# Parallel block (sliding attention and GEGLU): the first chunk reordered, stacks loaded sooner, another bank tag, an h tile loaded sooner

## The chip, the cores and the metric

The kernel runs on one core of one Trainium2 chip. A time is the device time of one execution in microseconds (us); the figure for a kernel is the median of its runs. In the profile PE is TensorE's matmuls, PEld its weight loads, DVE is VectorE, ACT ScalarE, POOL GpSimd, SP the engine that issues the DMAs (its queue is SPq). PEclk is the clock that TensorE was granted, 1.00 being full speed.

## The reference

A transformer block whose two branches run in parallel on one normalised input, in float32, with S = 2048 tokens, D = 640, 32 heads of 20, and a hidden width of 1728:

```python
xn = _layernorm(x, axis=-1)
return x + _A_ref(xn, A_wqkv, A_wo) + _B_ref(xn, B_w_gate, B_w_up, B_w_down)

# A: attention, each query sees the 256 latest keys
qkv = (xn @ wqkv).reshape(B, S, 3, H, Dh).transpose(2, 0, 3, 1, 4)
scores = einsum("bhqd,bhkd->bhqk", q, k) * Dh ** -0.5
mask = (idx[:, None] - idx[None, :] >= 0) & (idx[:, None] - idx[None, :] < 256)
p = softmax(where(mask, scores, -1e9));  a = (p @ v) @ wo
# B: GEGLU
h = gelu(xn @ w_gate) * (xn @ w_up);     b = h @ w_down
```

## The kernel before

Every dense product in float32 is made of three: an operand is split into a high part (rounded by ACT to TensorE's fast float format) and a low part (the rest, by a subtraction on DVE or GpSimd), and high·high, low·high and high·low are summed in one bank of PSUM (`dense_steps`, L79 to L84). So nearly every tile costs an ACT copy, a subtraction, and three matmuls for each block of 128.

The work is staged. Tokens are taken in four chunks of 512 (four tiles `xi` of 128 tokens).

1. **First chunk** (`first_chunk`, from L286): statistics of each tile on DVE (L119 to L121), variance plus epsilon (`ve`, L126), square root on ACT (`sq`, L127), a short DVE chain for the reciprocal root (L132 to L135), the normalisation (`ln_apply`, L139), the transposes on PE (`turn`, L156), then the high half of the transposed tile `xh` on ACT (L292) and the low half `xl` on DVE (L289). The chunk goes in two halves of 256 tokens, `ta` from tiles 0 and 1, `tb` from tiles 2 and 3. Meanwhile the weights of q and k of the first column blocks (`wr0`, `wr5`) are split: `wqh` on ACT (L74), `wql` on GpSimd (L75). PE's products are grouped in `part` (L296), five matmuls each. The weights of v are split as they come (`wvh`, L238, ACT; `wvl`, L239, GpSimd), and then come the projections `proj_v` and `proj_qk` (L82). Each projection of q or k is stored by `save_qk`: the evictions L215 and L216, L203 on ACT, the subtraction `pt` on GpSimd (L204, two buffers), and its stores on SP (L210).
2. **Chunks 1 to 3**: `ln_scale` (L141), `ln_turn`, `proj_v` and `proj_qk` of the chunk before. The statistics of chunk 1 are taken inside the first chunk.
3. **Attention** (`attention`): 32 units, one for each group of four heads and each chunk, of 14 slots each. In each slot the schedule issues score products, maxima, exponentials, the products with v, and some matmuls of a list of filler (the rest of the q, k and v projections, and gate and up products `gate_up_fill`). `load_stack` (L390) loads a unit's stacks of q (`qs`, three buffers) and k (`ks`, four buffers) from DRAM by six DMAs; `max_end` stores the maxima into the stack of q (L427).
4. **Gate and up products** of the remaining columns (`gate_up` and `gate_up_pair`), where products of sums of x and weights save some matmuls. Results `he` go to DRAM (`hd`) by L884 and L886.
5. **Down and output projections** (`terms`, L941): `load_step` (L900) loads an h tile, `split_step` splits it (L918 on ACT, L920 on GpSimd).

The order on PE, ACT and DVE is the order of the program in most of this (`manual_schedule` with the engines of `MANUAL`, SP too in stages 4 and 5); on an engine that isn't named there, GpSimd and SP in the stages before, a scheduler places the instructions. Before the change the attention's loads stand at the start of a unit:

```python
for u in range(NU + 1):
    if 1 <= u and u + 2 < NU:
        load_stack(u + 2)
```

The pool `psg` gives each tag ("g0" to "g3", two buffers each) its place in PSUM; the pools of the attention that held the same banks are closed before, so the first product in a bank waits for the bank's last reader.

Of the kernel before, what the change touches and what calls it, by code (L numbers as in the profile page):

```python
# [9 lines left out]
F32 = mybir.dt.float32  # L10
F32R = mybir.dt.float32r
BF = mybir.dt.bfloat16
AF = mybir.ActivationFunctionType
OP = mybir.AluOpType
# [31 lines left out]
def block_kernel(ctx, tc, x, xt, wqk, wv, wo, wgu, wd, wdl, out):  # L46
# [3 lines left out]
    dram = ctx.enter_context(tc.tile_pool(name="dram", bufs=1, space=DRAM))  # L50

    one = const.tile([128, 96], F32, name="one")
    nc.vector.memset(one, 1.0)
    nc.scalar.activation(one, one, AF.Sqrt)
    ident = const.tile([128, 128], F32, name="ident")
    make_identity(nc, ident)
    edge = ctx.enter_context(tc.tile_pool(name="edge", bufs=1, side="right"))
# [39 lines left out]
    vp = pr.enter_context(tc.tile_pool(name="vp", bufs=5, side="right"))  # L97
    st1 = pr.enter_context(tc.tile_pool(name="st1", bufs=1, side="right"))
    identb = st1.tile([128, 256], BF, name="identb")[:, 0:128]
    mask = st1.tile([128, 384], F32, name="mask")  # L100
    nc.gpsimd.memset(mask, 0.0)
    nc.gpsimd.affine_select(out=mask, in_=mask, pattern=[[1, 384]], compare_op=OP.is_ge,
# [14 lines left out]
    def ln_stats(xi, mv, lp):  # L117
        st = lp.tile([128, 2, 6], F32, name="st", tag="st", bufs=4)
        nc.vector.bn_stats(st[:, 0, :], xi[:, 0:320])  # L119
        nc.vector.bn_stats(st[:, 1, :], xi[:, 320:640])  # L120
        nc.vector.bn_aggr(mv, st)  # L121

    def ln_sqrt(mv, n, lp):
        ve = lp.tile([128, n], F32, name="ve", tag="ve", bufs=2)
        sq = lp.tile([128, n], F32, name="sq", tag="sq", bufs=2)
        nc.vector.tensor_scalar(ve, mv[:, :, 1], EPS, None, op0=OP.add)  # L126
        nc.scalar.activation(sq, ve, AF.Sqrt)  # L127
        return ve, sq

    def ln_rstd(ve, sq, n, lp):  # L130
# [154 lines left out]
    def first_chunk(xs, wr0, wr5, lp):  # L285
        halves = slice(0, 256), slice(256, 512)  # L286

        def low(k, ps, cs):
            nc.vector.tensor_tensor(out=xl[:, k, cs], in0=ps, in1=xh[:, k, cs].bitcast(F32), op=OP.subtract)  # L289

        def high(k, ps, cs):
            nc.scalar.activation(xh[:, k, cs], ps, AF.Copy)  # L292

        def part(ps, w, r, cs, first=False, last=False):
            for k in range(KT):
                nc.tensor.matmul(ps[:, cs], w[:, k, :], r[:, k, cs], start=first and k == 0,  # L296
                                 stop=last and k == KT - 1, skip_group_check=True)

        with tc.manual_schedule(engines=MANUAL):
            mv = [lp.tile([128, 2, 2], F32, name="mv", tag="mv", bufs=2) for _ in range(2)]  # L300
            ln_stats(xs[0], mv[0][:, 0, :], lp)
            ln_stats(xs[1], mv[0][:, 1, :], lp)
            va = ln_sqrt(mv[0], 2, lp)
            ln_stats(xs[2], mv[1][:, 0, :], lp)
            rs = ln_rstd(*va, 2, lp)
            ln_apply(xs[0], mv[0][:, 0, :], rs[:, 0:1])
            ln_apply(xs[1], mv[0][:, 1, :], rs[:, 1:2])
            ln_stats(xs[3], mv[1][:, 1, :], lp)
            w0 = split_qk(wr0)
            w5 = split_qk(wr5)  # L310
            ta = [turn(k, xs[0:2], "xmxmm"[k]) for k in range(KT)]
            dn = [psd.tile([128, C], F32, name="ps_d", tag="dn") for _ in range(2)]
            for k in range(KT):
                high(k, ta[k], halves[0])
                if k == 1:
                    vb = ln_sqrt(mv[1], 2, lp)
            for k in range(2):
                low(k, ta[k], halves[0])
            rs = ln_rstd(*vb, 2, lp)
            ln_apply(xs[2], mv[1][:, 0, :], rs[:, 0:1])  # L320
            ln_apply(xs[3], mv[1][:, 1, :], rs[:, 1:2])
            part(dn[0], w0[0], xh, halves[0], True)
            part(dn[1], w5[0], xh, halves[0], True)
            part(dn[0], w0[1], xh, halves[0])
            tb = [turn(0, xs[2:4], "o")]
            for k in range(2, KT):
                low(k, ta[k], halves[0])
            for k in range(1, 3):
                tb.append(turn(k, xs[2:4], "oxmxm"[k]))
            part(dn[1], w5[1], xh, halves[0])  # L330
            for k in range(3, KT):
                tb.append(turn(k, xs[2:4], "oxmxm"[k]))
            for k in range(KT):
                high(k, tb[k], halves[1])
            for k in range(KT):
                low(k, tb[k], halves[1])
            mv = lp.tile([128, 4, 2], F32, name="mv4", tag="mv4", bufs=2)
            for i, w in enumerate((w0, w5)):
                part(dn[i], w[0], xl, halves[0])
                part(dn[i], w[0], xh, halves[1])  # L340
                part(dn[i], w[1], xh, halves[1])
                part(dn[i], w[0], xl, halves[1], last=True)
                for j in range(2):
                    ln_stats(xs[4 + 2 * i + j], mv[:, 2 * i + j, :], lp)
                save_qk(5 * i, 0, dn[i])
        return w0, w5, mv

    v0 = []
    with tc.tile_pool(name="lp", bufs=1, side="right") as lp:
        xs = [ln_load(t, lp) for t in range(4)]  # L350
        warm = lp.tile([128, 256], BF, name="warm")[:, 0:128]
        nc.vector.memset(warm, 0.0)
        ps = psd.tile([128, C], F32, name="ps_u", tag="dn")
        for i in range(WARM):
            nc.tensor.matmul(ps[:, 0:128], warm, warm, start=True, stop=True)
        wr0, wr5 = load_qk(0), load_qk(5)
        prep = load_v(0, v0, lp)
        next(prep)
        xs += [ln_load(t, lp) for t in range(4, 8)]
        w0, w5, mv1 = first_chunk(xs, wr0, wr5, lp)  # L360
        nc.vector.tensor_copy(identb, ident)
        run(prep)
        v0 = v0[0]
        ones = lp.tile([2, 2 * C], BF, name="ones")
        nc.gpsimd.memset(ones, 1.0)
        for i in range(NK):
            for j in (0, 2):
                nc.sync.dma_start(ks[i][120:122, j:j + 2].rearrange("p j t -> p (j t)"), ones)
        for c in range(1, NC):
            ln_scale(xs[4 * c:4 * c + 4], lp, mv1 if c == 1 else None)  # L370
            ln_turn(4 * c, xs[4 * c:4 * c + 4])
            if c + 1 < NC:
                xs += [ln_load(t, lp) for t in range(4 * c + 4, 4 * c + 8)]
            if c == 2:
                raws1 = [load_qk(1), load_qk(6)]
            if c < NC - 1:
                run(*[proj_v(v0, 4 * c - 4 + i, None if i % 2 else (pso, "o")) for i in range(4)])
                run(proj_qk(0, w0, c), proj_qk(5, w5, c))
# [296 lines left out]
    def attention():  # L675
        now[0] = -1
        load_stack(0)
        load_stack(1)
        load_stack(2)
        for i, (p, k, half) in enumerate((p, k, half) for p in range(NC // 2) for k in range(2) for half in range(2)):  # L680
            for j, fn in enumerate(x_sums(p, k, half)):
                at(XS0 + XSN * i + 2 * j, fn)
        for i in range(12):
            now[0] = i - 13
            for fn, a in tick():
                fn(*a)
            for _ in range(2):
                pull_max(1, now[0])
                pull_fill(RAMP)
        pull_fill(GAP)  # L690
        for u in range(NU + 1):
            if 1 <= u and u + 2 < NU:
                load_stack(u + 2)
            for i in range(NS):
                T = now[0] = NS * u + i
                for fn, a in tick():
                    fn(*a)
                if i == 0 and u:
                    av_unit(u - 1)
                if i % 2 == 0:  # L700
                    if u < NU and i < 12:
                        exp_piece(u, i)
                        exp_piece(u, i + 1)
                    pull_max(3 if i in (6, 12) else 2, T)
                pull_fill(RATE / NS)
        while acts:
            now[0] += 1
            for fn, a in tick():
                fn(*a)
        now[0] = None  # L710
        run(fill)
        assert not acts
# [247 lines left out]
    for fn in w_sums(raws_w, sums):  # L960
        fn()
    w = tiles, sums
    gate_up(rest[0], 1, "g0")
    split_xs(0, 2, xraw[2])
    xraw[4] = load_xs(0, 4)
    gate_up(rest[0], 3, "g1")
    split_xs(0, 1, xraw[1])
    later = {2: load_xs(1, 2)}
    gate_up(rest[0], 0, "g2")
    split_xs(0, 3, xraw[3])  # L970
    later[1] = load_xs(1, 1)
    gate_up(rest[0], 2, "g3")
# [48 lines left out]
    for j, f in enumerate(range(NFA, NF - 1)):  # L1021
# [33 lines left out]
        if end:  # L1055
            for n in range(2):
                load_step(n)
            second[1].append(lambda: split_step(0))
            second[2].append(lambda: split_step(1))
        gate_up_pair(f, w, 1, second)  # L1060
        if end:
            load_step(2)
        else:
            w = nxt_w[0], sums
    order.__exit__(None, None, None)
    order = tc.manual_schedule(engines=MANUAL_OUT)
# [72 lines left out]
```

## Time and profile before

| | |
|---|---|
| median of 3 runs | 1113.44 us (1112.27 to 1115.75) |
| the profiled execution | 1111.94 us |
| its span | 1110.2 us |
| granted TensorE clock, mean | 0.998 |
| PE busy | 1091.4 us, 98% |
| DVE, ACT, POOL busy | 54%, 42%, 37% |
| first chunk | to about 24.5 us |
| chunks 1 to 3 | to about 64 us |
| attention with its filler | to about 660 us |
| gate and up products | to about 845 us |
| down and output projections | to the end |

A timeline row gives start and busy time in us, engine, line, operation, tile written and read, their shapes and the number of instructions grouped in the row; in brackets stands the engine's idle time ahead of it and what ended that. A row of waits gives the line that waited, what it waited for, and the waits' total, number and longest.

### The profile page before, as it was taken

Reading aid. Unit: us, or ns where it says so; the run is one execution under the profiler, and the core shown is the slowest. Engines: PE = TensorE matmul, PEld = TensorE weight load, DVE = VectorE, ACT = ScalarE, POOL = GpSimd, SP = SyncE. Lnnn points to the kernel's source line nnn. Section 1 sums busy time; section 2 is a strip of 40 time slices with the busy share of each in tenths; the row PEclk is TensorE's granted clock in tenths of the full one; section 3 lists DMA queues with packets and bytes.
Section 4 is the critical chain, followed back from the end, with each engine's and each line's share of the span. In section 5 each row is a group of like instructions: output and inputs, shape, how many; then the busy total and the mean of one; then the engine's idle time right before and its main releaser. Section 6 shows DMA issues by size and latency. Waiting matters only on the chain.

```text
span 1110.2 us, 19224 instructions
## 1 busy us (share of the span) xinstructions
PE 1091.4 (98%) x6778; PEld 831.3 (75%) x6778; DVE 602.4 (54%) x1646; ACT 469.2 (42%) x952; POOL 411.1 (37%) x568
## 2 busy tenths in 40 slices
PE   7999999999999999999999999999999999999998
PEld 7887666666678767666666768888887888788886
DVE  7856567565666566676666636666653350211203
ACT  4434655565644556554555555232233322211111
POOL 4144544566735435664424341111113313221230
PEclk9999999999999999999999999999999999999999
DMA  4642342446442233444333125122124735152431
GB/s 162 221 140 83 106 151 89 134 120 195 123 132 85 79 119 107 139 135 131 101 101 103 57 82 187 68 92 87 66 74 150 262 130 169 48 180 78 150 95 66
DMA packets 76144, 133.09 MB, mean 120 GB/s; under 512 B 12800, under 2 KB 33664, under 8 KB 76048
## 3 DMA queue, kind: packets, MB, share of 16 engines
q1 hardware_dynamic: 76048, 131.87, 37.7%
q8 instruction: 53, 0.87, 0.3%
q14 instruction: 43, 0.35, 0.1%
HBM read 86.31 MB, written 44.83 MB: 118 GB/s over the span
## 4 chain that ended last, share of the span: by engine, by line
PE 93%; DVE 3%; DMA 1%; ACT 1%; issue 1%; SPq 0%; POOL 0%; DVEq 0%; ACTq 0%
PE ps_d L82 25%; PE ps_w L941 22%; PE ps_g L850 15%; PE ps_o L484 7%; PE ps_e L462 7%; PE ps_m L410 7%; PE ps_v L82 6%; PE ps_g L82 1%; DVE junk L412 1%; PE ps_t L156 1%; PE ps_d L296 1%; DMA ks<-kd 0%; DMA xi<-x 0%; ACT P L464 0%; PE ps_b L911 0%
## 5 line engine op out<-in xcount | busy, mean ns | idle before, releaser
L412 DVE CUSTOM_DVE_ANT_0 junk<-ps_m,mask 128x384 bf16<-128x384 f32 (+2 forms) x512 | 271.8, 531 | 176.4 <-PE ps_m L410 135.3
L464 ACT ACTIVATE P<-ps_e 128x512 f32<-128x512 f32 (+2 forms) x384 | 197.6, 568 | 62.3 <-PE ps_e L462 55.4
L470 POOL TENSOR_SCALAR_AFFINE_SELECT P<-P 128x512 f32<-128x512 f32 x128 | 84.7, 662 | 174.6 <-ACT P L464 169.2
L920 POOL TENSOR_TENSOR ht<-hr,ht 128x512 fp32r<-128x512 f32 x52 | 69.5, 1342 | 173.2 <-ACT ht L918 173.2
L82 PE MATMUL ps_d<-xh,wql 128*128 128x512 f32 x430 | 129.2, 410 | 0.0
L82 PE MATMUL ps_d<-xl,wqh 128*128 128x512 f32 x430 | 128.6, 408 | 0.0
L82 PE MATMUL ps_d<-xh,wqh 128*128 128x512 f32 x430 | 128.5, 409 | 0.0
L410 PE MATMUL ps_m<-ks,qs 120*128 120x128 bf16 (+1 forms) x704 | 121.0, 275 | 3.3 <-DVE mx L412 2.2
L462 PE MATMUL ps_e<-qs,ks 122*128 122x128 bf16 (+2 forms) x704 | 112.9, 277 | 1.0 <-ACT P L464 0.4
L918 ACT ACTIVATE ht<-hr 128x512 fp32r<-128x512 f32 x56 | 35.1, 629 | 132.9 <-PE ps_w L941 80.7
L462 PEld LDWEIGHTS <-ks 122*128 122x128 bf16 x704 | 50.1, 98 | 54.3 <-issue 44.0
L82 PEld LDWEIGHTS ps_d<-xh,wql 128*128 128x128 f32 x430 | 77.9, 189 | 15.5 <-issue 1.9
L82 PEld LDWEIGHTS ps_d<-xl,wqh 128*128 128x128 f32 x430 | 78.2, 188 | 14.8 <-issue 0.4
L82 PEld LDWEIGHTS ps_d<-xh,wqh 128*128 128x128 f32 x430 | 77.8, 189 | 14.1 <-ACT xh L164 0.3
L410 PEld LDWEIGHTS <-qs 120*128 120x128 bf16 x704 | 62.0, 98 | 32.8 <-issue 13.3
L473 POOL TENSOR_SCALAR_AFFINE_SELECT P<-P 128x512 f32<-128x512 f32 x112 | 72.2, 655 | 35.1 <-ACT P L464 35.1
L484 PE MATMUL ps_o<-P,v 128*32 128x384 f32 (+2 forms) x1408 | 84.3, 386 | 0.0
L204 POOL TENSOR_TENSOR pt<-r,pt 128x512 bf16<-128x512 f32 x40 | 46.7, 1166 | 83.0 <-ACT pt L203 80.2
L484 PEld LDWEIGHTS ps_o<-P,v 128*32 128x32 f32 x1408 | 40.1, 110 | 39.5 <-issue 29.2
L75 POOL TENSOR_TENSOR wql<-wr,wqh 128x640 fp32r<-128x640 f32 x11 | 17.8, 1626 | 135.8 <-PE ps_g L850 106.1
L922 DVE TENSOR_TENSOR ht<-hr,ht 64x512 fp32r<-64x512 f32 x4 | 2.8, 691 | 112.3 <-ACT ht L918 112.3
L488 ACT ACTIVATE ob<-ps_o 128x512 f32<-128x512 f32 x32 | 19.1, 597 | 103.6 <-PE ps_o L484 53.2
(269 smaller groups left out, 2040.2 us busy)
## 6 DMA issues: line engine op xcount, KB each, us to landing
hd<-he SPq DMA_DIRECT2D x52, 256.0 KB
hr<-hd SPq DMA_DIRECT2D x52, 256.0 KB
wr<-wgu SPq DMA_DIRECT2D x27, 320.0 KB
qs<-qd SPq DMA_DIRECT2D x32, 240.0 KB
ks<-kd SPq DMA_DIRECT2D x32, 240.0 KB
xi<-x SPq DMA_DIRECT2D x16, 320.0 KB
qs<-qd SPq DMA_DIRECT2D x32, 160.0 KB
ks<-kd SPq DMA_DIRECT2D x32, 160.0 KB
```

The costliest lines, as they stand in the source:

```text
L82: nc.tensor.matmul(ps, a(k), b(k), start=n == 0, stop=n == 3 * nk - 1)
L204: nc.gpsimd.tensor_tensor(out=pt[:, l, :], in0=r, in1=pt[:, 1, :], op=OP.subtract)
L410: nc.tensor.matmul(ps[:, lo:hi], lh, rhs, start=True, stop=True)
L412: nc.vector.tensor_tensor_reduce(out=junk[:, 0:n], in0=ps[:, 0:n], in1=mask[:, 384 - n:384], scale=1.0, scalar=NEG, op0=OP.add, op1=OP.max ...
L462: nc.tensor.matmul(ps[:, col:col + n], k[0:QROWS, j, kc:kc + 128], q[0:QROWS, j, q0:q0 + n], start=True, stop=True)
L464: nc.scalar.activation(pt[:, j, lo:hi], ps[:, lo:hi], AF.Exp, scale=SCALE)
L470: nc.gpsimd.affine_select(out=a, in_=a, pattern=[[0, 4], [1, 128]], compare_op=OP.is_ge, fill=0.0, base=0, channel_multiplier=-1)
L473: nc.gpsimd.affine_select(out=a, in_=a, pattern=[[0, 4], [-1, 128]], compare_op=OP.is_ge, fill=0.0, base=-1, channel_multiplier=1)
L484: nc.tensor.matmul(o[32 * j:32 * j + 32, q0:q0 + n], v[:, w0_:w0_ + 32], pt[:, j, col:col + n], start=i == 0, stop=i == len(todo) - 1, ski ...
L850: nc.tensor.matmul(ps, i, j, start=first and n == 0, stop=n == len(work) - 1, skip_group_check=True)
L920: nc.gpsimd.tensor_tensor(out=t[:, 1, :], in0=raw, in1=t[:, 0, :].bitcast(F32), op=OP.subtract)
L941: nc.tensor.matmul(pss[m], w[:, ms], r, start=first and j == 0, stop=last and j == len(work) - 1)
```

## The change

Four edits.

*First chunk.* The epsilon gets a tile of its own (a part of the constant tile `one`). The square root takes the variance itself, with the epsilon as its bias, while `ve` is made by an addition of two tiles. The statistics of tiles 2 and 3 move behind the normalisation of tiles 0 and 1. ACT's evictions and weight copies are interleaved in a new order, with the second square root behind the third eviction. GpSimd's order is written out too in this function, and its subtractions `wql` stand behind a copy of one column of the normalised fourth tile into `one`. On PE the transposes of the second half go ahead of all the products with `wql`, and those ahead of the last. The bfloat16 copy of the identity moves from DVE to GpSimd, and to the program's start.

*Stacks.* `load_stack(u + 3)` is called in slot 11 of unit u, where `load_stack(u + 2)` was called at slot 0 of unit u (so a unit's stacks are asked for three slots sooner).

*Bank.* The first `gate_up` uses the tag "g2" and the third "g0".

*h tile.* `load_step(2)` is called before the last product of the last `gate_up_pair` rather than behind that function.

```diff
-    nc.vector.memset(one, 1.0)
-    nc.scalar.activation(one, one, AF.Sqrt)
+    nc.vector.memset(one[:, 0:92], 1.0)
+    nc.scalar.activation(one[:, 0:92], one[:, 0:92], AF.Sqrt)
+    eps = one[:, 92:96]
+    nc.vector.memset(eps, EPS)
...
+    nc.gpsimd.tensor_copy(identb, ident)
...
-        nc.vector.tensor_scalar(ve, mv[:, :, 1], EPS, None, op0=OP.add)
-        nc.scalar.activation(sq, ve, AF.Sqrt)
+        nc.vector.tensor_tensor(out=ve, in0=mv[:, :, 1], in1=eps[:, 0:n], op=OP.add)
+        nc.scalar.activation(sq, mv[:, :, 1], AF.Sqrt, bias=eps[:, 0:1])
...
+        def high_qk(raw):
+            wh = wp.tile([128, KT, 128], F32R, name="wqh", tag="wqh")
+            nc.scalar.activation(wh, raw, AF.Copy)
+            return wh
+
+        def low_qk(raw, wh):
+            wl = wp.tile([128, KT, 128], F32R, name="wql", tag="wql")
+            nc.gpsimd.tensor_tensor(out=wl, in0=raw, in1=wh.bitcast(F32), op=OP.subtract)
+            return wh, wl
+
-        with tc.manual_schedule(engines=MANUAL):
+        with tc.manual_schedule(engines=MANUAL | {mybir.EngineType.Pool}):
             mv = [lp.tile([128, 2, 2], F32, name="mv", tag="mv", bufs=2) for _ in range(2)]
             ln_stats(xs[0], mv[0][:, 0, :], lp)
             ln_stats(xs[1], mv[0][:, 1, :], lp)
-            va = ln_sqrt(mv[0], 2, lp)
-            ln_stats(xs[2], mv[1][:, 0, :], lp)
-            rs = ln_rstd(*va, 2, lp)
+            rs = ln_rstd(*ln_sqrt(mv[0], 2, lp), 2, lp)
             ln_apply(xs[0], mv[0][:, 0, :], rs[:, 0:1])
             ln_apply(xs[1], mv[0][:, 1, :], rs[:, 1:2])
+            ln_stats(xs[2], mv[1][:, 0, :], lp)
             ln_stats(xs[3], mv[1][:, 1, :], lp)
-            w0 = split_qk(wr0)
-            w5 = split_qk(wr5)
             ta = [turn(k, xs[0:2], "xmxmm"[k]) for k in range(KT)]
             dn = [psd.tile([128, C], F32, name="ps_d", tag="dn") for _ in range(2)]
-            for k in range(KT):
+            high(0, ta[0], halves[0])
+            wh0 = high_qk(wr0)
+            high(1, ta[1], halves[0])
+            wh5 = high_qk(wr5)
+            high(2, ta[2], halves[0])
+            vb = ln_sqrt(mv[1], 2, lp)
+            for k in (3, 4):
                 high(k, ta[k], halves[0])
-                if k == 1:
-                    vb = ln_sqrt(mv[1], 2, lp)
...
-            part(dn[0], w0[0], xh, halves[0], True)
-            part(dn[1], w5[0], xh, halves[0], True)
-            part(dn[0], w0[1], xh, halves[0])
+            part(dn[0], wh0, xh, halves[0], True)
+            part(dn[1], wh5, xh, halves[0], True)
+            nc.gpsimd.tensor_copy(one[:, 0:1], xs[3][:, 0:1])
+            w0, w5 = low_qk(wr0, wh0), low_qk(wr5, wh5)
             tb = [turn(0, xs[2:4], "o")]
             for k in range(2, KT):
                 low(k, ta[k], halves[0])
-            for k in range(1, 3):
-                tb.append(turn(k, xs[2:4], "oxmxm"[k]))
-            part(dn[1], w5[1], xh, halves[0])
-            for k in range(3, KT):
+            for k in range(1, KT):
                 tb.append(turn(k, xs[2:4], "oxmxm"[k]))
...
+            part(dn[0], wh0, xl, halves[0])
+            part(dn[1], wh5, xl, halves[0])
+            part(dn[0], wh0, xh, halves[1])
+            part(dn[1], wh5, xh, halves[1])
             for i, w in enumerate((w0, w5)):
-                part(dn[i], w[0], xl, halves[0])
-                part(dn[i], w[0], xh, halves[1])
+                part(dn[i], w[1], xh, halves[0])
                 part(dn[i], w[1], xh, halves[1])
                 part(dn[i], w[0], xl, halves[1], last=True)
...
-        nc.vector.tensor_copy(identb, ident)
...
-            if 1 <= u and u + 2 < NU:
-                load_stack(u + 2)
...
+                if i == 11 and 3 <= u + 3 < NU:
+                    load_stack(u + 3)
                 pull_fill(RATE / NS)
...
-    gate_up(rest[0], 1, "g0")
+    gate_up(rest[0], 1, "g2")
...
-    gate_up(rest[0], 0, "g2")
+    gate_up(rest[0], 0, "g0")
...
+            second[3].append(lambda: load_step(2))
         gate_up_pair(f, w, 1, second)
-        if end:
-            load_step(2)
-        else:
+        if not end:
             w = nxt_w[0], sums
```

## The prediction

> **What bounds the kernel now.** I read the page's busy shares and the shares of the chain that ended last, then TensorE's waits by their releaser, then the timeline around each of those waits.
>
> ```profile
> span 1110.2 us, 19224 instructions
> PE 1091.4 (98%) x6778; PEld 831.3 (75%) x6778; DVE 602.4 (54%) x1646; ACT 469.2 (42%) x952; POOL 411.1 (37%) x568
> PE 93%; DVE 3%; DMA 1%; ACT 1%; issue 1%; SPq 0%; POOL 0%; DVEq 0%; ACTq 0%
> ```
>
> ```profile
> PE ps_t L156 <- DVE xi L139: 3.8, 3, 2.7
> PE ps_d L296 <- ACT xh L292: 3.5, 1, 3.5
> ...
> PE ps_m L410 <- DMA ks<-kd: 0.8, 1, 0.8
> PE ps_g L82 <- DVE he L549: 0.8, 1, 0.8
> PE ps_w L941 <- POOL ht L920: 0.6, 1, 0.6
> PE ps_w L941 <- ACT ht L918: 0.6, 1, 0.6
> ```
>
> TensorE is busy 98% of the span and carries 93% of the chain, so the products themselves, which the change leaves alone, are the time. Only 1110.2 − 1091.4 = 18.8 us are not PE's. The second block lists waits as total, times, longest. Its six rows sum to 10.1 us, and the change touches the place of nearly all of it. So the most that it can bring is these 10.1 us, plus what a slowed TensorE clock costs behind an idle stretch. About 0.3% (3.3 us) is what a measurement of this kernel can tell from no change, so the whole case is played in a few microseconds.
>
> **Part 1, the first chunk.**
>
> ```profile
> 6.23 0.17 DVE L126 TENSOR_SCALAR ve<-mv 128x2 f32<-128x2 f32 x1
> 6.43 0.20 ACT L127 ACTIVATE sq<-ve 128x2 f32<-128x2 f32 x1 [4.06 <-DVE ve L126]
> ...
> 7.79 0.11 DVE L132 RECIPROCAL rs<-sq 128x2 f32<-128x2 f32 x1
> ...
> 8.53 1.14 DVE L139 TENSOR_SCALAR xi<-xi,mv,rs 128x640 f32<-128x640 f32 x2
> ...
> 9.26 3.30 POOL L75 TENSOR_TENSOR wql<-wr,wqh 128x640 fp32r<-128x640 f32 x2 [6.34 <-DMA wr<-wqk]
> 9.29 1.64 PE L156 MATMUL ps_t<-ident,xi 128*128 128x128 f32 x10 [2.69 <-DVE xi L139]
> ...
> 11.31 2.77 DVE L126 TENSOR_SCALAR ve<-mv 128x2 f32<-128x2 f32 x1
> ...
> 14.23 0.92 ACT L292 ACTIVATE xh<-ps_t 128x256 fp32r<-128x256 f32 x3
> ...
> 14.65 1.56 PE L296 MATMUL ps_d<-xh,wqh 128*128 128x256 f32 x5 [3.47 <-ACT xh L292]
> ...
> 24.53 0.90 PE L82 MATMUL ps_v<-wvh,xh 128*128 128x320 f32 x5
> ```
>
> The first square root ends at 6.63, but the reciprocal runs at 7.79, because the statistics of the third tile stand between them on DVE. The change moves these behind the two applies, and lets the root read the variance itself (its bias carries the epsilon), so that it no longer waits for the 0.17 us addition. My estimate is the reciprocal at 6.47, the applies from 7.26, and the first transposes at 8.02 instead of 9.29: 1.27 us.
>
> The second wait is the larger one. The addition `ve` on 128x2 numbers took 0.17 us once and 2.77 us the second time, while the two GpSimd subtractions `wql` (1.65 us each) ran. ACT's second root stood behind that addition, and three evictions `xh` behind the root, so PE idled 3.47 us. After the change the subtractions are held back behind a copy that reads the fourth normalised tile, the root reads only the variance, and it stands behind three of the evictions. The first half's evictions then end at about 11.65 rather than 15.15.
>
> [...]
>
> ```profile
> 14.00:16.00 2.00, 1.35 (x5) 1.26 (x6) 1.59 (x9) 1.88 (x7) 0.55 (x3) 0.74 0.01 2
> 16.00:18.00 2.00, 2.00 (x11) 2.00 (x11) 2.00 (x4) 0.58 (x2) 2.00 (x4) 0.50 0.05 14
> 18.00:20.00 2.00, 2.00 (x18) 2.00 (x17) 1.09 (x4) 1.60 (x6) 1.62 (x3) 0.90 0.03 8
> ```
>
> These are windows of 2 us; the number after the five engines' busy times is TensorE's granted clock. Behind the 3.47 us of idleness it was 0.74, 0.50 and 0.90, which lost (0.26 + 0.50 + 0.10) × 2 = 1.72 us of full speed. The new order leaves PE no idle stretch as long, so I count on most of this coming back.
>
> What becomes late next is GpSimd. In the built order three subtractions of the v weights still go ahead of the holding copy, so the two `wql` come out at about 17.3 and 18.9 by my walk (1.65 us each, behind the apply of the fourth tile at 13.2 to 14.1). The products that don't need them were put ahead of them on PE. All that need the second one and the rest then end at 20.9 to 21.3, at worst 22.0. The v projection, which starts at 24.53 before, starts 3.2 to 3.6 us sooner (2.5 at worst). The copy of the identity leaves DVE for GpSimd's idle start. The eight small stores of ones move from behind the stores on SP to about 7 us, where SP has only loads already issued; I cost both at nothing, and if SP were late there, a tile of chunk 2 would come later, which has some 15 us to spare.
>
> Part of this is lost again at the next chunk.
>
> ```profile
> 27.03 1.17 POOL L204 TENSOR_TENSOR pt<-r,pt 128x512 bf16<-128x512 f32 x1 [1.47 <-ACT pt L203]
> 27.30 0.93 DVE L133 TENSOR_TENSOR ve<-ve,rs 128x4 f32<-128x4 f32 x1
> ...
> 28.65 1.66 DVE L139 TENSOR_SCALAR xi<-xi,mv,rs 128x640 f32<-128x640 f32 x3
> ...
> 29.32 0.66 PE L156 MATMUL ps_t<-ident,xi 128*128 128x128 f32 x4 [0.67 <-DVE xi L139]
> ```
>
> Chunk 1's transposes come off DVE's chain, not off PE's. I estimate its first apply at 26.0 to 26.5 and the transposes at 26.7 to 27.2 instead of 29.32, that is 2.1 to 2.6 us sooner. PE has by then done six more matmuls of the v projection (five span 0.74 us from issue to issue, so 0.88). The gain of part 1 is 3.0 to 3.5 by this walk. I take 3.0; its bounds are 1.0 (both DVE chains stretched by GpSimd, as at 27.30) and 3.5.
>
> **Part 2, the loads of q and k.**
>
> ```profile
> SPq L210 <- POOL pt L204: 116.7, 35, 10.1
> ```
>
> ```profile
> 250.71 0.69 SPq L427 DMA_DIRECT2D qs<-mr  x1
> ...
> 252.23 1.16 POOL L204 TENSOR_TENSOR pt<-r,pt 128x512 bf16<-128x512 f32 x1 [2.03 <-ACT pt L203]
> 253.42 2.25 SPq L210 DMA_DIRECT2D qd<-pt  x3
> ...
> 256.96 1.08 SPq L390 DMA_DIRECT2D ks<-kd  x3
> ...
> 263.12 0.33 PE L410 MATMUL ps_m<-ks,qs 120*128 120x128 bf16 x2 [0.80 <-DMA ks<-kd]
> ```
>
> In SP's order the six loads of a unit now stand right behind the store of the maxima (L427), ahead of the projection stores (L210). Here they would be issued from 251.40 instead of from 255.76, some 4.4 us sooner, so the one wait of 0.80 us goes. I take 0.8, between 0 (the next maximum then waits for DVE instead) and 0.9. The price: three loads took 1.08 us to issue, so six take 2.2, and the store behind them can issue at 253.65 instead of 253.42. Elsewhere SP waits 116.7 / 35 = 3.3 us on average for GpSimd's `pt` at that line, so on average the six issues lie inside that wait. The other 28 or so loads that are moved were never waited for; they bring nothing.
>
> **Part 3, the bank.**
>
> ```profile
> 659.52 0.69 DVE L549 SCALAR_TENSOR_TENSOR he<-gs,ps_d 128x512 f32<-128x512 f32 x1 [3.43 <-PE ps_d L82]
> ...
> 660.26 1.43 PE L82 MATMUL ps_g<-xh,wqh 128*128 128x512 f32 x5 [0.78 <-DVE he L549]
> ```
>
> The first product of the next stage waits 0.78 us for the last reader of the bank it is put in. The change renames the tags, but the pool hands out banks in the order in which tags are first asked for. So "g2", asked for first, gets the bank that "g0" had, and the built program indeed places it there. I take 0; if the bank did change, 0.8 to 1.1 would go.
>
> **Part 4, the third h tile.**
>
> ```profile
> 839.94 2.54 POOL L920 TENSOR_TENSOR ht<-hr,ht 128x512 fp32r<-128x512 f32 x2 [5.04 <-ACT ht L918]
> ...
> 847.90 2.57 SPq L900 DMA_DIRECT2D hr<-hd  x2
> ...
> 851.92 0.39 PE L941 MATMUL ps_w<-ht,wd1h 128*128 128x512 f32 x1
> ...
> 852.22 0.63 ACT L918 ACTIVATE ht<-hr 128x512 fp32r<-128x512 f32 x1 [6.72 <-DMA hr<-hd]
> ...
> 852.92 2.53 POOL L920 TENSOR_TENSOR ht<-hr,ht 128x512 fp32r<-128x512 f32 x2 [10.44 <-ACT ht L918]
> ...
> 856.43 0.62 PE L941 MATMUL ps_w<-ht,wd2h 128*128 128x512 f32 x2
> ```
>
> The load issued at 847.90 stands behind the stores of the last products on SP. Its tile reaches ACT at 852.22 and GpSimd at 852.92, and PE waits 0.6 us for each. Moved ahead of those stores, it is issued once the slot is free, about 841.3 (half of the 2.54 us behind 839.94). With the 4.3 us that it took here it lands near 845.6, and the subtraction ends near 847.5, well before PE asks at 852.3. From 851.92 to 856.43 PE issued 12 matmuls in 4.51 us; at the pace of 0.62 − 0.39 = 0.23 each they need 2.76. That is 1.75 us lost, 1.2 by the two gaps alone. I take 1.6. The two stores behind it are read only by the thirteenth step of the projection.
>
> **Sum.** −3.0 − 0.8 − 0 − 1.6 = −5.4. The profiled execution took 1111.94 us, 1.74 over its span and 1.50 under the median of 1113.44; it becomes 1106.5, and the median 1108.0.
>
> **The rivals.**
> *The stores pay for the loads* (the other side). A projection store that is ready sooner than SP is idle for 2.2 us now waits behind six issues; its `pt` buffer, of which there are two, comes free later, then ACT's eviction, the dense bank and PE. It decides from the point where SP's wait at L210 falls under 2.2 us. The mean of 3.3 speaks against it, the spread (up to 10.1 in one) for it. If five of the 35 had no slack at all, it would cost 5 × 2.2 = 11 us: 1119. Chance 0.09.
> *The gain is given back at chunk 1.* GpSimd's `pt` and v-weight subtractions meet DVE's short chain again, as in 0.93 against 0.16 us, and stretch the applies; part 1 is worth 1.0 only: 1110.0. [...] Chance 0.16.
> *The clock drops again.* The first chunk keeps idle stretches of 1 to 2 us; if they fall so that a window is granted 0.50, up to 1.7 us go: 1109.7. [...] Chance 0.14.
> *Nearly nothing arrives*: part 1 is worth 1.0 and part 2 and 4 half: 1111 to 1112.5. Chance 0.09.
> *The bank does change*: 1107.0. Chance 0.03.
>
> **How the numbers follow.** The forecast itself keeps 0.49. Faster by over 0.3% means under 1110.1: the forecast, the bank, two thirds of the clock's case and about half of chunk 1's, with room: 0.70. Slower by over 0.3%, above 1116.8, is the stores' case with a little for what I have not seen: 0.10. The rest, 0.20, is within 0.3%. The range runs from 1105.0 (every part at its upper bound, 3.5 + 0.9 + 1.1 + 1.75 = 7.3, with a little of the clock) to 1112.5, where nearly nothing arrives; outside it lie the stores' case and the unforeseen.
>
> **What would show it.** Right: first transposes near 8.0, no idle of over 2 us on PE and no clock of 0.50 before 20 us, the v projection's start at 21 to 22, transposes of chunk 1 near 27; no wait of L410 on `ks`; still a wait of about 0.8 on `he` at the first product of the next stage; no wait on `ht` near 850. Wrong: a second root that still ends late, PE waits on `ps_d` in the attention with ACT's evictions late behind `pt` stores, or a v projection that starts no sooner than 23.

## The result and the profile after

The changed kernel took 1110.57 us (median of 10 runs, 1109.08 to 1111.76) against 1113.39 us of the kernel before (10 runs too): a ratio of 0.9973, with a 95% interval of 0.9964 to 0.9983. It is faster by 2.8 us, about half of the 5.4 us forecast, and just under the 3.3 us that were called measurable there. The profiled execution took 1110.84 us with a span of 1109.1.

First the head of after's page (span and busy shares), then TensorE's waits: total, times, longest.

```profile
span 1109.1 us, 19240 instructions
PE 1092.0 (98%) x6778; PEld 830.3 (75%) x6778; DVE 600.4 (54%) x1646; ACT 468.8 (42%) x952; POOL 410.5 (37%) x570
```

```profile
PE ps_t L159 <- DVE xi L142: 3.1, 4, 1.3
...
PE ps_w L955 <- POOL ht L934: 1.5, 2, 0.7
PE ps_m L424 <- DVE nm L431: 1.5, 1, 1.5
...
PE ps_g L84 <- DVE he L563: 0.8, 1, 0.8
PE ps_d L299 <- ACT xh L295: 0.5, 1, 0.5
```

The wait of 3.5 us on `xh` is down to 0.5, the wait on `ks` at L410 and the two on the third h tile are gone. But two rows are new: 1.5 us on `nm` in the attention, and 1.5 us on `ht` in the last stage. They are what the forecast missed.

The timeline of after's first chunk:

```profile
6.33 0.30 ACT L130 ACTIVATE sq<-mv,one 128x2 f32<-128x2 f32 x1 [3.95 <-DVE mv L124]
...
8.20 1.63 PE L159 MATMUL ps_t<-ident,xi 128*128 128x128 f32 x10 [1.34 <-DVE xi L142]
...
11.06 0.30 ACT L130 ACTIVATE sq<-mv,one 128x2 f32<-128x2 f32 x1
...
12.19 1.69 DVE L142 TENSOR_SCALAR xi<-xi,mv,rs 128x640 f32<-128x640 f32 x2
12.36 3.07 POOL L242 TENSOR_TENSOR wvl<-wvall,wvh 128x320 fp32r<-128x320 f32 x3 [7.49 <-DMA ks<-ones]
...
13.93 1.20 PE L159 MATMUL ps_t<-ident,xi 128*128 128x128 f32 x9 [0.74 <-DVE xi L142]
...
15.52 3.11 POOL L309 TENSOR_TENSOR wql<-wr,wqh 128x640 fp32r<-128x640 f32 x2
...
20.96 0.90 PE L84 MATMUL ps_v<-wvh,xh 128*128 128x320 f32 x5
...
26.75 0.66 PE L159 MATMUL ps_t<-ident,xi 128*128 128x128 f32 x4 [0.79 <-DVE xi L142]
```

The second root runs at 11.06 rather than 14.12, the v projection starts at 20.96 rather than 24.53, and chunk 1's transposes run at 26.75 rather than 29.32. The first maxima of the attention start 3.65 us sooner (60.38 against 64.03).

From there I kept a ledger: the same matmul's start before minus its start after, wherever that lead changes. It is 3.65 at first; less 0.35 in the tenth unit; plus 0.9 at the twelfth unit (the wait on `ks` is gone), less 0.3 just behind; less 1.4 at the twenty-fourth unit; less 0.65 in two steps, at 596 and 602 us of after. At the end of the attention 1.9 is left. The third h tile gives 1.75, the ninth takes 1.06 and the thirteenth 1.5. At the last matmul the lead is 1.1 us, which is what separates the two spans. The medians are 2.8 apart because the execution of before that was profiled took 1111.94 us, 1.5 less than the median on record with the forecast, and that of after took 0.3 more than its median. The last 0.65 is not shown to be the change's: e3 and e9 below lose it too, with neither the stacks' edit nor a lead, and e1 doesn't lose it. The two large losses are these two places of after's timeline:

```profile
464.08 0.78 SPq L213 DMA_DIRECT2D kd<-pt  x2
464.95 1.37 SPq L404 DMA_DIRECT2D qs<-qd  x3
466.37 1.09 SPq L404 DMA_DIRECT2D ks<-kd  x3
...
472.62 0.33 PE L424 MATMUL ps_m<-ks,qs 120*128 120x128 bf16 x2 [1.48 <-DVE nm L431]
```

```profile
869.28 0.74 ACT L76 ACTIVATE wd10h<-wr 128x640 fp32r<-128x640 f32 x1 [2.73 <-DMA wr<-wd]
869.92 0.62 ACT L932 ACTIVATE ht<-hr 128x512 fp32r<-128x512 f32 x1
...
872.07 0.74 PE L955 MATMUL ps_w<-ht,wd8h 128*128 128x512 f32 x2 [0.75 <-POOL ht L934]
...
884.64 0.74 ACT L76 ACTIVATE wo1h<-wr 128x640 fp32r<-128x640 f32 x1 [2.09 <-DMA wr<-wo]
885.28 0.61 ACT L932 ACTIVATE ht<-hr 128x512 fp32r<-128x512 f32 x1
...
885.95 0.50 PE L955 MATMUL ps_w<-ht,wd12h 128*128 128x512 f32 x1 [0.21 <-ACT ht L932]
...
887.43 0.74 PE L955 MATMUL ps_w<-ht,wd12h 128*128 128x512 f32 x2 [0.74 <-POOL ht L934]
```

In the first, the stack loads of the twenty-fourth unit stand behind a late projection store of k, and the matmul that needs them waits (the row names `nm`, which that matmul doesn't read; the next section shows that moving the loads takes the wait away). In the second, ACT copies the ninth h tile only behind `wd10h`, the weights of two steps later, which had to wait 2.73 us for their DMA; likewise the thirteenth tile behind `wo1h`.

### The profile page after: what moved, and what is told of

Same layout as the page of the kernel before. It is cut to its first block, busy times and chain, and to the rows that moved or that the text cites. A ratio compares the mean times of both kernels' runs of the same rounds, so it can differ in the third digit from the quotient of the medians.

```text
span 1109.1 us, 19240 instructions
## 1 busy us (share of the span) xinstructions
PE 1092.0 (98%) x6778; PEld 830.3 (75%) x6778; DVE 600.4 (54%) x1646; ACT 468.8 (42%) x952; POOL 410.5 (37%) x570
## 4 chain that ended last, share of the span: by engine, by line
PE 85%; DVE 5%; issue 3%; DMA 2%; ACT 2%; POOL 1%; SPq 1%; DVEq 0%; POOLq 0%; ACTq 0%
PE ps_d L84 23%; PE ps_w L955 19%; PE ps_g L864 14%; PE ps_o L498 7%; PE ps_e L476 7%; PE ps_m L424 7%; PE ps_v L84 5%; DVE junk L426 2%; PE ps_g L84 1%; POOL ht L934 1%; ACT P L478 1%; DVE xi L142 1%; PE ps_t L159 1%; DMA hr<-hd 1%; DVE r L219 0%
## 5 line engine op out<-in xcount | busy, mean ns | idle before, releaser
L84 PEld LDWEIGHTS ps_d<-xh,wqh 128*128 128x128 f32 x430 | 77.7, 189 | 14.1 <-ACT xh L167 0.3
L77 POOL TENSOR_TENSOR wql<-wr,wqh 128x640 fp32r<-128x640 f32 x9 | 14.5, 1615 | 129.5 <-PE ps_g L864 106.1
```

Source lines behind the costliest of these rows:

```text
L84: nc.tensor.matmul(ps, a(k), b(k), start=n == 0, stop=n == 3 * nk - 1)
```

## The experiments

The ratios are to the kernel before, timed on the same chip; intervals are of 95%.

**e1: the first chunk alone.** Before, with the change's edits of the first chunk and nothing else.

> Before with the first chunk's new order alone. Theory A (ledger of the two traces): the first chunk is worth 3.3 to 3.6 us, all of it stays to the end, so about 1109.9 median (0.9969). Rival B (the lead shifts everything by some us and is partly lost to new DMA waits in the attention): a lead of 3.4 at the attention's start, but 1 to 2 us less at the end, about 1111.3. The wait of 0.8 on ks and the two waits on the third h tile (1.75 us with their restart) must be there again, and no wait at the later h tiles.

Measured: 0.9979 (0.9970 to 0.9989), 1111.21 us, runs from 1108.86 to 1112.84. In its profile the lead is 3.4 at the start of the attention and 3.1 at the last matmul; the profiled run was the fastest of the ten. The trace bears out theory A; the median, 1.9 us below before, is nearer to B, and the interval (1.2 to 3.3 us) leaves 3.4 just outside. One thing expected did not come: the wait on `ks` at the twelfth unit is 0.18 us here, not 0.8, though the loads are called where they were before. And at the twenty-fourth unit TensorE waits 0.67 us, so the lead alone costs something there. What separates the execution profiled from the others is looked at under "clock" below.

**e2: the stacks alone.**

```diff
-            if 1 <= u and u + 2 < NU:
-                load_stack(u + 2)
...
+                if i == 11 and 3 <= u + 3 < NU:
+                    load_stack(u + 3)
```

> Before with the stacks loaded three slots sooner alone. Theory A: the wait of 0.8 on ks at the twelfth unit goes (0.7 to 0.9 gained) and nothing else; the wait of 1.5 at the twenty-fourth unit, seen in the trace after, comes by chance or only with the first chunk's lead, so about 1112.6 (0.9993). Rival B: the loads sooner cause that wait, because they crowd the DMA queues for the loads behind a late projection store; then the wait of 1.5 is in this trace too and the time is 1113.4 to 1114 (1.000 to 1.0005).

Measured: 1.0007 (0.9999 to 1.0016), 1113.74 us. Rival B's time, and its wait is in the trace, though without the first chunk's lead:

```profile
467.11 0.79 SPq L210 DMA_DIRECT2D kd<-pt  x2
468.00 1.37 SPq L390 DMA_DIRECT2D qs<-qd  x3
469.41 1.09 SPq L390 DMA_DIRECT2D ks<-kd  x3
...
475.48 0.33 PE L410 MATMUL ps_m<-ks,qs 120*128 120x128 bf16 x2 [1.30 <-DMA od<-ob]
```

Here the row names a DMA. Before, these six loads were issued by 470.63 and the matmul ran at 475.17, with 0.08 us of waiting: this unit had no margin. In e2 TensorE is there 0.9 us sooner, the loads are issued by 470.50, hardly sooner, and the matmul runs 4.98 us after them. So most of the loss is the wait of the twelfth unit, moved to the next place without margin; that the landing took 0.4 us longer as well is seen and not explained. The change's promise, three slots sooner, was not kept for this unit, because SP stands at the store of k until GpSimd has made `pt` (465.93 to 467.09).

**e3: the h tile alone.**

```diff
+            second[3].append(lambda: load_step(2))
         gate_up_pair(f, w, 1, second)
-        if end:
-            load_step(2)
-        else:
+        if not end:
```

> Before with the third h tile loaded sooner alone. Theory A: the earlier load takes away the two waits on the third h tile (1.75 us), but the scheduler, which orders ACT in the last stage, now places each h tile's copy one weight copy later; the copies of the ninth and the thirteenth h tile then stand behind weights that come late, and cost 1.0 and 1.5 us: in all 0.8 us slower, 1114.2 (1.0007). Rival B (the prediction's): 1.6 us faster, 1111.8 (0.9986), the late waits in the trace after having come by chance.

Measured: 0.9993 (0.9984 to 1.0002), 1111.93 us. The time is rival B's, and the interval leaves theory A's 1.0007 outside; the trace has something of both. It gains the 1.75 us at the third tile and loses 0.6 at the ninth and next to nothing at the thirteenth. This row has the larger part of the 0.6:

```profile
874.79 0.73 PE L941 MATMUL ps_w<-ht,wd8h 128*128 128x512 f32 x2 [0.35 <-POOL ht L920]
```

ACT's built order is the same here as in after (`wd9h`, `wd10h`, ninth tile; `wo0h`, `wo1h`, thirteenth tile), and in the kernels without this edit it is another (the ninth tile ahead of `wd9h`). So the edit makes the order, and how late the weights land in an execution decides what the order costs. Five traces have both the edit and this order: the third tile gives 1.75 us in each, and the ninth and thirteenth take 0.4 (e5), 0.6 (here), 0.9 (e7), 2.6 (after) and 3.8 (e10).

**e4: after without the h tile's edit.**

> After with the third h tile's load put back. Theory A: 0.8 us faster than after, 1109.8 (0.9967); the waits at the ninth and thirteenth h tile are gone and the two at the third are back. Rival B: 1.6 us slower than after, 1112.2.

Measured: 0.9978 (0.9969 to 0.9987), 1110.09 us. Its trace has the two waits at the third tile again and none at the ninth and thirteenth, as theory A said; the times of after (0.9973) and of this can't be told apart. By those five traces the edit is worth between 1.4 us faster (e5) and 2.1 slower (e10).

**e5: the loads ahead of the store.** In after, the call of the loads goes ahead of slot 11's deferred work.

```diff
+                if i == 11 and 3 <= u + 3 < NU:
+                    load_stack(u + 3)
                 for fn, a in tick():
                     fn(*a)
...
-                if i == 11 and 3 <= u + 3 < NU:
-                    load_stack(u + 3)
```

> After, with the stack loads called ahead of the deferred work of slot 11 instead of behind it; in the built order this moves the six loads of the twenty-fourth unit ahead of a late projection store of k, and hardly anything else. Theory A (that unit's loads are no sooner than before, because they queue behind that store, while TensorE comes 0.9 us sooner): the wait of 1.2 to 1.5 us at that unit goes, about 1.2 us faster than after, 1109.3. Rival B (the landing itself is slow there, whatever the order, for want of DMA room): the wait stays and the time is after's, 1110.5.

Measured: 0.9972 (0.9959 to 0.9984), 1108.96 us where before took 1112.23; the profiled run was the fastest of the six. SP in its trace, at the same unit:

```profile
460.47 1.15 SPq L404 DMA_DIRECT2D qs<-qd  x3
461.67 1.08 SPq L404 DMA_DIRECT2D ks<-kd  x3
463.97 0.81 SPq L213 DMA_DIRECT2D kd<-pt  x2
...
470.55 0.66 PE L424 MATMUL ps_m<-ks,qs 120*128 120x384 bf16 x4
```

The loads are issued 4.5 us sooner, ahead of the store, and TensorE goes on without a wait: the lead keeps its 4.3 us through this unit. So the loads' place behind the store made the 1.48 in after. A slower landing beside it is not ruled out, since an issue 4.5 us sooner would hide that as well. The gain of 1.4 us is shown by the trace; the ratio alone, beside after's, would not show it.

**e6: ACT's order in the last stage.** In after, ACT is added to the engines with a written order there, and each tile's split goes ahead of the weight split of its step.

```diff
-    order = tc.manual_schedule(engines=MANUAL_OUT)
+    order = tc.manual_schedule(engines=MANUAL_OUT | {mybir.EngineType.Activation})
```

> After, with ACT's order in the last stage written out: each h tile's copy ahead of the weight copy of the same step. Theory A (the late waits on the ninth and thirteenth h tile come from copies placed behind late weights): none of these waits in the trace, 0.5 to 2.5 us faster than after, about 1109.2. Rival B (the h tiles' loads themselves are late, since on SP they stand behind weight loads that wait for a buffer): the waits stay, 1110.5. Another order can also bring a new wait of ACT for a tile that is not free: slower.

Measured: 0.9967 (0.9955 to 0.9980), 1108.31 us. From 840 us on the trace has no wait of TensorE at all; the lead rises by 1.75 at the third tile and stays. Theory A.

**e7: really another bank.** In after, the four tags are asked for in their old order first, and the first product uses the third tile.

```diff
+    pg4 = [psg.tile([128, C], F32, name="ps_g", tag=f"g{i}") for i in range(4)]
-    gate_up(rest[0], 1, "g2")
+    gate_up(rest[0], 1, pg4[2])
```

> After, with the four tags of the first gate and up products asked for in the old order ahead of their use, so that the first product really lands in another bank. Theory A: the wait of 0.8 on he goes and 0.8 to 1.1 us stay to the end: 1109.5. Rival B: the next product, or the next wait on that bank, takes it back: 1110.5.

Measured: 0.9969 (0.9956 to 0.9981), 1108.89 us.

```profile
658.04 1.33 PE L84 MATMUL ps_g<-xh,wqh 128*128 128x512 f32 x5
658.24 0.69 DVE L563 SCALAR_TENSOR_TENSOR he<-gs,ps_d 128x512 f32<-128x512 f32 x1 [3.44 <-PE ps_d L84]
```

The product now starts 0.2 us ahead of the reader that it used to wait for; the lead grows by 0.93 and keeps it. So in after the rename did nothing, as forecast, and a true change of bank is worth 0.9.

**e8: the three together.**

> After with the loads ahead, ACT's order and the bank of the three runs beside it together. Theory A: the gains add up, 2.5 to 4.5 us under after, 1106 to 1108. Rival B: each only uncovers the next wait, 1109 to 1110.

Measured: 0.9934 (0.9922 to 0.9946), 1105.22 us: 7.0 us under before, and clear of after's interval. In the traces the gains add: its lead at the last matmul is 6.7, 5.6 more than after's. The medians alone would not have shown any one of the three: by the ratios e5, e6 and e7 lie 0.1 to 0.7 us under after, each within its interval.

**e9: only the root's operand.** Before, the root reads the variance (and the epsilon gets its tile, as in the change). In the first chunk the order of DVE and ACT stays.

```diff
-        nc.scalar.activation(sq, ve, AF.Sqrt)
+        nc.scalar.activation(sq, mv[:, :, 1], AF.Sqrt, bias=eps[:, 0:1])
```

> Before, with nothing but the square root reading the variance (epsilon as its bias) instead of the sum; the order on every engine stays. Theory A (the wait of 3.5 us was ACT's root standing behind a DVE addition that GpSimd held up): the second root runs near 11.4 instead of 14.1, the wait of 3.5 on ps_d falls under 1.0, the clock of 0.50 behind it goes, and the v projection starts 1.5 to 3 us sooner than 24.5: about 1110.5 against 1112.5 for before. Rival B (DVE's addition itself, still held to 14.1, sets the start of the second half's transposes): the wait moves to those transposes, and under 1 us is gained.

Measured: 1.0023 (1.0015 to 1.0032), 1115.88 us: slower.

```profile
8.19 2.38 DVE L141 TENSOR_SCALAR xi<-xi,mv,rs 128x640 f32<-128x640 f32 x2
8.68 3.30 POOL L77 TENSOR_TENSOR wql<-wr,wqh 128x640 fp32r<-128x640 f32 x2 [5.77 <-ACT wqh L76]
...
11.28 2.27 DVE L363 CAST identb<-ident 128x128 bf16<-128x128 f32 x1
...
11.98 1.57 DVE L123 BATCH_NORM_AGGREGATE mv<-st 128x2 f32<-128x12 f32 x1
12.46 1.01 POOL L367 MEMSET ones<- 2x1024 bf16 x1
...
13.61 0.30 ACT L129 ACTIVATE sq<-mv,one 128x2 f32<-128x2 f32 x1 [1.97 <-DVE mv L123]
```

The root no longer waits for the addition, and still runs at 13.61, because other work of DVE ahead of it now takes longer beside GpSimd's: the applies 2.38 rather than 1.14, the cast 2.27 rather than 0.79, the last aggregate `mv` 1.57 rather than 0.20. The v projection starts at 24.68, no sooner than before. But this is not a clean test of the root. The two applies ran beside `wql`, which started at 8.68, just ahead of the second apply at 8.72; in the three other traces with the old order it started at 9.07 to 9.26, and in before, at 9.26 and so behind the second apply's start, both took 1.14. And behind the first chunk the built program differs in more than the root: from 26 us on ACT, from 36 us on DVE and SP, and from 100 us on GpSimd have some instructions in another order. So what the root alone is worth stays open, and why the median lost 2.9 us is only partly seen (in the profiled run, the second fastest of the twelve, 0.25 by the start of the attention and 1.5 in small steps through it).

**e10: after without the hold.**

```diff
-            nc.gpsimd.tensor_copy(one[:, 0:1], xs[3][:, 0:1])
-            w0, w5 = low_qk(wr0, wh0), low_qk(wr5, wh5)
...
+            w0, w5 = low_qk(wr0, wh0), low_qk(wr5, wh5)
             vb = ln_sqrt(mv[1], 2, lp)
```

> After, without the holding copy and with the two GpSimd subtractions wql called as soon as their weights are split (with the third eviction). Theory A (GpSimd keeps DVE from its second chain and applies): an operation of DVE between 10.5 and 14 us is stretched to over 1.5 us, the transposes of the second half come 1 to 3 us later than 13.9, and the time is 0.5 to 2.5 us over after. Rival B (it is the root's wait alone that mattered): the chain is stretched, but the products with wql can fill PE meanwhile, and the time is after's.

Measured: 1.0008 (0.9999 to 1.0017), 1113.9 us: 0.35% over after. The profiled run was the slowest of the eleven (1116.12).

```profile
10.01 3.07 POOL L309 TENSOR_TENSOR wql<-wr,wqh 128x640 fp32r<-128x640 f32 x2 [5.37 <-ACT wqh L304]
...
10.55 1.01 DVE L129 TENSOR_TENSOR ve<-mv,one 128x2 f32<-128x2 f32 x1
...
13.15 4.64 POOL L242 TENSOR_TENSOR wvl<-wvall,wvh 128x320 fp32r<-128x320 f32 x5
...
14.07 2.18 DVE L142 TENSOR_SCALAR xi<-xi,mv,rs 128x640 f32<-128x640 f32 x2
...
15.23 0.48 PE L159 MATMUL ps_t<-ident,xi 128*128 128x128 f32 x1 [2.38 <-DVE xi L142]
```

Three steps of DVE's chain take 1.01, 0.75 and 0.71 us instead of the 0.16 of each in after, and the two applies 2.18 instead of 1.69. The second half's transposes come 2.4 us later than in after (16.30 against 13.93), TensorE idles 2.38 us, and its granted clock is 0.50 from 14 to 20 us; the v projection starts at 25.19. Without the hold the whole gain of the first chunk is gone, by the median too. Theory A, at more than its price.

**e11: e8 with more warming matmuls** (76 for 64).

> The kernel of the three changes together (e8), with 76 instead of 64 warming matmuls at the start, which fill PE's idle time of 1.3 us ahead of the first transposes. Theory A (the executions differ because the idle stretches of the first chunk sometimes fall into a window that is then granted half the clock): fewer such executions, the median 0.3 to 0.8 under e8's (0.993 of before), the spread narrower. Rival B: the warming matmuls come out of PE's queue later than the transposes are ready, and cost 0.1 to 0.3.

Measured: 0.9945 (0.9933 to 0.9957), 1106.47 us. No gain: its profile still has a clock of 0.50 in the window of 14 to 16 us, though the idle stretch ahead of the first transposes was filled (TensorE busy for 2.00 us of the window of 6 to 8, 0.86 in after). Theory A fails: filling that stretch did not keep the clock up.

**e12: e8 with all low parts of v behind the two of q and k.**

> The kernel of the three changes together (e8), with all five v-weight subtractions on GpSimd behind the two wql, where three of them stood ahead of the holding copy. Theory A (GpSimd's three hold up DVE's applies of the third and fourth tile, 1.7 us for both instead of 1.1, and the wql come late): transposes of the second half 0.5 us sooner, the v projection 0.3 to 0.8 sooner, of which 0.3 to 0.5 stays. Rival B: they then run beside DVE's chain of chunk 1 and give it back, or PE waits for the low v weights near 22: no gain, or up to 1 us slower.

Measured: 0.9933 (0.9921 to 0.9945), 1106.03 us: the same as e8.

```profile
23.91 1.01 DVE L137 SCALAR_TENSOR_TENSOR ve<-ve,rs 128x4 f32<-128x4 f32 x1
...
26.42 0.66 PE L159 MATMUL ps_t<-ident,xi 128*128 128x128 f32 x4 [1.50 <-DVE xi L142]
```

The v projection starts 0.74 us sooner than in e8 (19.93 against 20.67), and chunk 1's transposes at 26.42 against 26.46: all of it is given back to DVE's chain of chunk 1, which sets these transposes, and where a step that takes 0.16 us in the first chunk took 1.01 beside GpSimd's `pt` (23.73 to 24.90), as in after. Rival B.

**Clock.** The executions of one kernel differ by some 3 us, and part of this is seen in the profiles. Windows of e7, to set beside after's:

```profile
14.00:16.00 2.00, 2.00 (x12) 2.00 (x10) 2.00 (x7) 1.73 (x5) 2.00 (x4) 0.50 0.08 17
16.00:18.00 2.00, 2.00 (x14) 2.00 (x13) 1.97 (x6) 0.00 (x0) 2.00 (x2) 0.65 0.27 47
```

```profile
14.00:16.00 2.00, 2.00 (x18) 2.00 (x19) 2.00 (x7) 1.49 (x5) 2.00 (x4) 1.00 0.05 14
16.00:18.00 2.00, 2.00 (x19) 2.00 (x18) 1.97 (x7) 0.00 (x0) 2.00 (x2) 1.00 0.85 232
```

With the same program of the first chunk, e7 got half the clock and after all of it. Of the nine profiles with the new first chunk and its hold, three (e6, e7, e11) have such a stretch and start the v projection at 21.8 to 22.2, the other six at 19.9 to 21.0. All four profiles with the old one (before, e2, e3, e9) have it, and so has e10.

The mean granted clock that is on record for every run says how often. It is 0.998 in the three profiles with the stretch and 0.999 or 1.000 in the six without, and it is 0.998 or less in 31 of the 62 runs of these nine kernels. Within a kernel those 31 took 1.2 us longer on average.

How long the half clock lasts can be worked out from the windows: in e7 the whole of 14 to 16 us and (1.00 − 0.65) × 2 / 0.50 = 1.40 of the next window, 3.4 us. In the same way it is 3.4 us in before, e2, e6, e9 and e11, 6.8 in e10 and 10.2 in e3, about one, two and three times the same length; in before it runs from 14.97 to 18.39. It starts at another time in each, about 12.9 us in e6, 13.7 in e11 and 14.0 in e7. Another change at the start of the program moves too: the warming matmuls, the same 64, go from 0.107 to 0.056 us each at 4.76 us in before and at 5.30 in after (on both sides the windows print 1.00). In e7 it comes later still: the window of 4 to 6 us has 22 matmuls, against 33 in before and 28 in after. What brings the half clock on is not shown. From 10 to 14 us, ahead of e7's drop, TensorE was busy for 1.41 and 1.25 us of each 2.00 in e7 as in e8, for 1.35 and 1.26 in after, and for 1.41 and 1.80 in e12; of these four only e7 was slowed.

## Why the prediction was right or wrong

**Part 1** was right in its walk: applies from 7.26 (7.45 measured), first transposes 8.02 (8.20), the first half's evictions done at 11.65 (11.92), the fourth tile's apply done at 14.1 (13.88), `wql` at 18.9 (18.6), v projection at 20.9 to 21.3 (20.96), chunk 1's transposes at 26.7 to 27.2 (26.75). The lead at the attention was 3.65 against 3.0 to 3.5. What carried it was the hold: without it the rest gains nothing (e10). The weight that I gave to the root's operand is not borne out: e9 shows no gain from it, and can't say what it is worth alone. The addition in the kernel before was also not held by `wql` alone. These end at 12.56; it ended at 14.08, when GpSimd's fill of `ones` did (14.06 in the timeline of before), which the change moves to the start:

```profile
13.05 1.01 POOL L365 MEMSET ones<- 2x1024 bf16 x1
```

Which forms of a DVE addition GpSimd's work stretches is not shown. The one that replaced it took 0.16 us at 10.65 in after, where GpSimd was idle, and 1.01 beside `wql` in e10.

**Part 2** failed in its bounds, "between 0 and 0.9". The wait of 0.8 went, as said, and came back as 1.1 to 1.6 at the twenty-fourth unit (after, e2, e4, e6, e7, e10); alone the edit measures 1.0007. The 0.8 itself was read from one trace: in e1 and e3, with the loads in their old place, that wait is 0.18 and 0.42. Two sentences were wrong: that the loads stand "ahead of the projection stores" (not at this unit, where a store of k stays ahead), and that the other loads "were never waited for". One of them had been waited for by 0.08 us, and a gain ahead of it was paid there, in part even without this edit (0.67 in e1).

**Part 3** was right: 0.78 us before and after, and e7 shows 0.9 for a true change, within the 0.8 to 1.1 named.

**Part 4** was right at its place, 1.75 us by the trace, and wrong in the sum: costed as if nothing else moved. One load called sooner made the scheduler place the later h tiles' copies, all but the twelfth's, behind one more weight copy (the sixth behind two), and 0.4 to 3.8 us were paid at the ninth and thirteenth tile.

**The sum** was −5.4, and −2.8 came. In the profiled executions it is 3.65 − 0.35 + 0.9 − 0.3 − 1.4 − 0.65 + 1.75 − 2.56 = 1.0, and with the rounding 1.1. Part 1 gave 3.65 for its 3.0, part 2 took 0.8 for a gain of 0.8 (0.9 − 0.3 − 1.4), part 4 took 0.8 for a gain of 1.6, and 1.0 went at places that no part names. So the step that failed is the same in parts 2 and 4: each was costed as if the rest of the kernel kept its order and its margins. That the time still lies in the range owes something to part 1 coming out above its upper bound; the 0.70 put on a gain of over 0.3% did not come (0.27%).

**The rivals:** the stores did not pay for the loads: the list of TensorE's waits has none on `ps_d` in the attention of after. The gain of the first chunk was not given back at chunk 1. The clock's drop was real and its chance of 0.14 too low: by the recorded clock it came in 31 of 62 runs, at 1.2 us on average, within the 1.7 put down. It is part of why medians gain less than the best profile (e1: 1.9 against 3.4).

## What to carry to other kernels

Where a scheduler places what is not ordered by hand, an edit at one place can reorder an engine far behind it: read the built order of every engine to the end, not only around the edit. Taking away a wait brings the whole rest of the kernel nearer to its loads, so look for the next place whose margin is smaller than the gain, and ask what each load is queued behind. When a short operation is stretched by a neighbour on another engine, move the neighbour (e10 shows what that is worth); in e9, freeing one waiting instruction left others stretched. An experiment that edits one line can change the built order elsewhere, so compare the orders before calling it a test of that line.

## What the runs showed of the hardware that was not expected

The same program was granted different clocks in the same window from one execution to the next (0.50 in e7, 1.00 in after, 14 to 16 us), with TensorE as busy ahead of it: 1.25 and 1.26 of 2.00 us in the window before. From the first transposes to 14 us no wait of TensorE was over 0.8 us in e7, and after's longest was 0.74; ahead of them after idled 1.34 us and e7 hardly at all (busy for 1.96 of the 2.00 us from 6 to 8), and it was e7 that was slowed. What decides between the two is not shown. Where the half clock came in the first chunk, in eight of the fourteen profiles, it lasted 3.4, 6.8 or 10.2 us.

Under e9 a DVE cast took 2.27 us instead of 0.79. It began at 11.28, beside a GpSimd subtraction that ended at 11.98, and ended at 13.55, when the 1.01 us fill of `ones` begun at 12.46, which reads nothing, was over (13.47).
